# Hand-written order on all engines, V on ScalarE's queue, the late weights behind step 2's V: linear attention and a gated spatial MLP on one core

## The chip, the cores and the metric

The kernel runs on one core of one Trainium2 chip. Times are device microseconds of one execution; the span in a profile is some 1.7 us shorter than the time of the same run. A run over 1.5 per cent above the fastest of its kernel is called slow and left out of ratios. A ratio is the mean time of one kernel's fast runs over that of the other's fast runs of the same rounds, so it is not quite the ratio of the medians quoted beside it.

## The reference, cut to what matters

```python
# attention: q, k, v are (4, 8, 768, 64) float32, lam is one decay per head
intra = (q_b @ k_b.T * Dmask) @ v_b            # inside a block
inter = (q_b * lam_pow) @ kv_state             # from all blocks before
kv_state = lam_block * kv_state + (k_b * rev_pow).T @ v_b
x = out.transpose(0, 2, 1, 3).reshape(4, 768, 512)
# gated MLP with a spatial product over the sequence
h = maximum(x @ w_in, 0)                       # (512, 1024)
u, v = h[..., :512], h[..., 512:]
v_n = (v - mean(v)) / sqrt(var(v) + 1e-6)
v_s = w_spatial @ v_n + b_spatial              # (768, 768) on the sequence
y = (u * v_s) @ w_out                          # (512, 512)
```

Four batches of three steps make twelve steps of 256 tokens. The spatial product of a batch needs all three steps of that batch. That is why the first batch cannot finish before its three steps of K, Q and V (4.7 MB) and the weights (2.95 MB, counted as bf16) have landed.

## The kernel before

Names used in all profile lines (line numbers such as L344 differ from kernel to kernel): `kd`, `qc`, `vc` are the bf16 casts of K (with decay), Q and V. `pt` holds their transposes, evicted as `kT` and `qT`. `pam` is the scores, masked into `a`; `pkv` goes into the state `s` by way of `sd`; `pat` is the attention output, evicted as `xT`. `pv` and `pu` are the two halves of the input projection, evicted as `vh` and `uT`; `st`, `mv`, `rstd`, `vn` are the LayerNorm. `pvs` is the spatial product, gated into `gT`, and `po` the output projection.

All of K, Q and V are issued by SyncE, step by step:

```python
    def load_step(n):
        ...
        for c in range(2):
            nc.sync.dma_start(out=k_in[:, :, c, :], in_=...)
        nc.sync.dma_start(out=q_in..., in_=...)
        for c in range(2):
            nc.sync.dma_start(out=v_in[:, :, c, :], in_=...)
```

Only TensorE and GpSimd are in a written order; a scheduler orders the rest. The weights are issued by GpSimd, all of them ahead of the third step's casts:

```python
    with tc.manual_schedule(engines={PE, mybir.EngineType.Pool}):
        cast_step(0)
        load_win(0, DH)
        cast_step(1)
        nc.gpsimd.dma_start(out=wsp_raw, ...)      # spatial weight
        nc.gpsimd.dma_start(out=bsp_bc, ...)
        nc.gpsimd.dma_start(out=wout_sb, ...)
        trans_step(0); scores_step(0); kv_step(0); trans_step(1)   # (four lines in the source)
        load_step(4)
        fills = {0: 1, 1: 2, 2: 5}
        for n in range(NS):
            if n + 2 < NS:
                cast_step(n + 2)
            ...                                   # loads, scores, output, projections as fills
```

Of the kernel before, what the change touches and what calls it, by code (L numbers as in the profile page):

```python
# [9 lines left out]
FP32 = mybir.dt.float32  # L10
BF16 = mybir.dt.bfloat16
I32 = mybir.dt.int32
AF = mybir.ActivationFunctionType
ALU = mybir.AluOpType
PE = mybir.EngineType.PE
# [3 lines left out]
def kernel(  # L19
# [12 lines left out]
    nc = tc.nc  # L32
    P = 128
    B, H, S, D = q.shape
# [21 lines left out]
    def two_banks(shape, name, dt=FP32):  # L56
        return psum.tile(shape, dt, tag="ps", name=name)


    lam_bc = const.tile([P, H], FP32)  # L60
    nc.scalar.dma_start(out=lam_bc, in_=lam.unsqueeze(0).to_broadcast((P, H)))

    st = {}

    def load_step(n):
        b, r = divmod(n, NR)
        toks = slice(r * T2, (r + 1) * T2)
        q_in = fin.tile([P, H, 2, D], FP32, tag="q_in", name=f"q_in_{n}")
        k_in = fin.tile([P, H, 2, D], FP32, tag="k_in", name=f"k_in_{n}")
        v_in = fin.tile([P, H, 2, D], FP32, tag="v_in", name=f"v_in_{n}")  # L70
        for c in range(2):
            nc.sync.dma_start(out=k_in[:, :, c, :],  # L72
                              in_=k[b, :, toks][:, c * P:(c + 1) * P].rearrange("h p d -> p h d"))
        nc.sync.dma_start(out=q_in.rearrange("p h m d -> p h (m d)"),  # L74
                          in_=q[b, :, toks].rearrange("h (p m) d -> p h (m d)", m=2))
        for c in range(2):
            nc.sync.dma_start(out=v_in[:, :, c, :],  # L77
                              in_=v[b, :, toks][:, c * P:(c + 1) * P].rearrange("h p d -> p h d"))
        st[n] = {"q_in": q_in, "k_in": k_in, "v_in": v_in}

    load_step(0)
    ident = const.tile([P, P], BF16)
    make_identity(nc, ident)

    def iota_f(shape, pattern, base, mult, name):
        ti = const.tile(shape, I32, name=name + "_i")
        nc.gpsimd.iota(ti, pattern=pattern, base=base, channel_multiplier=mult)
        tf = const.tile(shape, FP32, name=name)
        nc.vector.tensor_copy(out=tf, in_=ti)
        return tf  # L90

    krev = iota_f([P, 1], [[0, 1]], P - 1, -1, "krev")

    qpos = iota_f([P, 2, 2, D], [[1, 2], [0, 2], [2, D]], 1, 0, "qpos")

    rel = iota_f([P, 2, D], [[1, 2], [2, D]], 0, -1, "rel")

    win_sb = wpool.tile([P, NCH, DFF], BF16)
    wout_sb = wpool.tile([P, NCH, DM], BF16)
    bsp_bc = wpool.tile([P, S], BF16)  # L100
    wt_sb = wpool.tile([P, NBLK, S], BF16)
    wsp_raw = wpool.tile([P, NBLK, S], BF16)

    def load_win(f0, f1):
        nc.gpsimd.dma_start(out=win_sb[:, :, f0:f1],
                            in_=moe_w_in.rearrange("(g p) f -> p g f", p=P)[:, :, f0:f1])

    load_win(DH, DFF)
    for n in range(1, 4):
        load_step(n)  # L110


    loglam = const.tile([P, H], FP32)
    nc.scalar.activation(out=loglam, in_=lam_bc, func=AF.Ln)
# [3 lines left out]
        nc.vector.tensor_copy(out=logl[rows, :], in_=loglam[rows, hh::2])  # L118
    ldec = const.tile([P, H], FP32)
    nc.scalar.activation(out=ldec, in_=loglam, func=AF.Exp, scale=krev[:, 0:1])  # L120
    lq = const.tile([P, NG, T2], BF16)
    for g in range(NG):
        nc.scalar.activation(out=lq[:, g, :], in_=qpos.rearrange("p m a d -> p (m a d)"),
                             func=AF.Exp, scale=logl[:, g:g + 1])
    l128 = const.tile([P, NG], FP32)
    nc.scalar.activation(out=l128, in_=logl, func=AF.Exp, scale=float(P))
    lm128 = const.tile([P, H], FP32)
    nc.scalar.activation(out=lm128, in_=loglam, func=AF.Exp, scale=-float(P))
    causal = const.tile([P, P], FP32)
    nc.vector.tensor_scalar(out=causal, in0=rel.rearrange("p m d -> p (m d)"), scalar1=0.0,  # L130
                            scalar2=None, op0=ALU.is_ge)
    amask = const.tile([P, 2, 2, 2, P], FP32)
    for h in range(H):
        nc.vector.tensor_scalar(out=amask[:, h // 4, h % 2, (h // 2) % 2, :], in0=causal,
                                scalar1=lm128[:, h:h + 1], scalar2=None, op0=ALU.mult)
    eps_t = const.tile([P, 1], FP32)
    nc.vector.memset(eps_t, 1e-6)
    oo128 = const.tile([P, P], BF16)
    nc.vector.memset(oo128, 1.0 / P)


    xT = {}

    def cast_step(n):
        s = st[n]
        kd = att.tile([P, 2, H, D], BF16, tag="kd", name=f"kd_{n}")
        qc = att.tile([P, 2, H, D], BF16, tag="qc", name=f"qc_{n}")
        vc = att.tile([P, H, 2, D], BF16, tag="vc", name=f"vc_{n}")
        eng = nc.vector if n < NR else nc.gpsimd
        eng.tensor_tensor(out=kd.rearrange("p c h d -> p h c d"), in0=s["k_in"],  # L150
                          in1=ldec.unsqueeze(2).unsqueeze(3).broadcast_to((P, H, 2, D)),
                          op=ALU.mult)
        nc.scalar.activation(out=qc.rearrange("p m h d -> p h m d"), in_=s["q_in"], func=AF.Copy)  # L153
        nc.gpsimd.tensor_copy(out=vc, in_=s["v_in"])  # L154
        s["kd"], s["qc"], s["vc"] = kd, qc, vc

# [112 lines left out]
    def pv(b, r):  # L269
        if r == 0:  # L270
            gmlp_tiles(b)
        x, m = xT[b], gm[b]
        vh, mv, rstd = m["vh"], m["mv"], m["rstd"]
        ps = two_banks([P, 2, DH], f"pv_{b}_{r}")
        for j in range(2):
            for c in range(NCH):
                nc.tensor.matmul(out=ps[:, j], lhsT=x[:, r, c, j * P:(j + 1) * P],  # L277
                                 rhs=win_sb[:, c, DH:DFF], start=(c == 0), stop=(c == NCH - 1))
        pair = slice(2 * r, 2 * r + 2)
        nc.scalar.activation(out=vh[:, pair, :], in_=ps, func=AF.Relu)  # L280
        for t in (2 * r, 2 * r + 1):
            nc.vector.bn_stats(out=m["st6"][:, t, :], in_=vh[:, t, :])  # L282
            nc.vector.bn_aggr(out=mv[:, t, :], in_=m["st6"][:, t, :])
        nc.scalar.activation(out=rstd[:, pair], in_=mv[:, pair, 1], func=AF.Sqrt,
                             bias=eps_t[:, 0:1])
        nc.vector.reciprocal(out=rstd[:, pair], in_=rstd[:, pair])
        for t in (2 * r, 2 * r + 1):
            nc.vector.tensor_scalar(out=m["vn"][:, t, :], in0=vh[:, t, :],  # L288
                                    scalar1=mv[:, t, 0:1], scalar2=rstd[:, t:t + 1],
                                    op0=ALU.subtract, op1=ALU.mult)  # L290
# [45 lines left out]
        nc.scalar.activation(out=wt_sb[:, s:s + 2, :], in_=ps[:, :, 0:S], func=AF.Copy)  # L336


    pend = []

    def fill(n):
        for _ in range(min(n, len(pend))):
            pend.pop(0)()

    def after_out(n):
        b, r = divmod(n, NR)
        pend.append(lambda: pv(b, r))
        if r == 0:
            pend.append(lambda: pu(b, 0))
        if r == NR - 1:  # L350
            pend.append(lambda: pu(b, 1))
            pend.append(lambda: pu(b, 2))
            if b == 0:
                pend.extend([lambda s=s: wt_piece(s) for s in (0, 2, 4)])
            pend.extend([lambda f=f: pvs(b, f) for f in range(NCH)])
            pend.extend([lambda i=i: po(b, i) for i in range(NR)])

    with tc.manual_schedule(engines={PE, mybir.EngineType.Pool}):
        cast_step(0)
        load_win(0, DH)  # L360
        cast_step(1)
        nc.gpsimd.dma_start(out=wsp_raw, in_=moe_w_spatial.rearrange("(a p) s -> p a s", p=P))
        nc.gpsimd.dma_start(out=bsp_bc, in_=moe_b_spatial.unsqueeze(0).to_broadcast((P, S)))
        nc.gpsimd.dma_start(out=wout_sb, in_=moe_w_out.rearrange("(t p) f -> p t f", p=P))
        trans_step(0)
        scores_step(0)
        kv_step(0)
        trans_step(1)
        load_step(4)
        fills = {0: 1, 1: 2, 2: 5}  # L370
        for n in range(NS):
            if n + 2 < NS:
                cast_step(n + 2)
            if n + 5 < NS:
                load_step(n + 5)
            if n + 1 < NS:
                scores_step(n + 1)
            out_step(n)
            after_out(n)
            if n + 1 < NS:  # L380
                kv_step(n + 1)
            f = fills.get(n, 4 + (n % 3 == 0))
            fill(f // 2)
            if n + 2 < NS:
                trans_step(n + 2)
            fill(f - f // 2)
        fill(len(pend))


# [28 lines left out]
```

## Time and profile before

| | kernel before |
|---|---|
| median of the first 4 runs | 185.78 us (185.46 to 186.53) |
| span in the profile | 186.7 us (of a longer run, 188.46 us) |
| V of step 2 cast by GpSimd | 42.0 us, after a wait of 14.4 us |
| first spatial product without a stop (S below) | 66.5 us |
| last matmul ends | 181.5 us |
| work of TensorE per batch at full clock | 33.4 us |

Read it from the middle. From 80 us on TensorE is busy in nearly every slice, so only the opening, up to the first spatial product, has anything large to give. The prediction below shows the lines.

### The profile page before, as it was taken

The numbers are of one execution on the slowest core, as the hardware profiler recorded it, in microseconds if no ns is written. First come the engines' busy times: TensorE is split into PE (matmuls) and PEld (weight loads), VectorE is DVE, ScalarE is ACT, GpSimd is POOL, SyncE is SP. The second block draws the span as 40 slices with busy tenths as digits, with TensorE's granted clock in tenths as the row PEclk, the third lists the DMA queues.
The fourth block names the chain that finished last, engine by engine and source line by source line (L and its number), as shares of the span: only waits on it lengthen the run. The fifth ranks groups of instructions, "written<-read, shape, count | busy, mean of one in ns | idle before, by whom it ended". The sixth has DMA issues, their size and how long they took to land.

```text
span 186.7 us, 3638 instructions
## 1 busy us (share of the span) xinstructions
PE 145.7 (78%) x1540; PEld 96.5 (52%) x1540; DVE 103.4 (55%) x191; ACT 89.1 (48%) x98; POOL 34.8 (19%) x35
## 2 busy tenths in 40 slices
PE   0005677507979779999997999999799999999980
PEld 0005563305649556655776665575676646565430
DVE  1029993705399853542989747169884722564400
ACT  4244324712677942268775613666722157660051
POOL 4004060006245344060606005020000000000000
PEclk9999996975999979999999999999999999999999
DMA  4999969999999999999998900530000027000035
GB/s 98 218 211 252 205 161 184 199 212 232 199 241 248 200 239 238 221 225 222 330 254 195 252 8 0 208 133 4 0 0 4 2 79 262 0 0 4 0 132 205
DMA packets 68337, 28.36 MB, mean 152 GB/s; under 512 B 50528, under 2 KB 65248, under 8 KB 68320
## 3 DMA queue, kind: packets, MB, share of 16 engines
q1 hardware_dynamic: 65664, 25.17, 56.5%
q0 software_dynamic: 2512, 2.95, 9.6%
q8 instruction: 12, 0.20, 0.5%
q14 instruction: 5, 0.04, 0.1%
q10 hardware_dynamic: 144, 0.00, 0.0%
HBM read 24.78 MB, written 6.29 MB: 166 GB/s over the span
## 4 chain that ended last, share of the span: by engine, by line
PE 54%; SPq 13%; DVE 11%; ACT 9%; DMA 9%; issue 2%; POOL 1%; ACTq 0%; POOLq 0%
PE pvs L307 17%; PE po L322 11%; DMA v_in<-in_v_dram 9%; PE pv L277 8%; PE pu L297 7%; SPq L77 6%; SPq L72 5%; PE pt L163 4%; DVE a L192 3%; PE pvs L309 3%; SPq L74 3%; DVE st L282 3%; ACT vh L280 2%; ACT wt_sb L336 2%; DVE vn L288 2%
## 5 line engine op out<-in xcount | busy, mean ns | idle before, releaser
L307 PE MATMUL pvs<-wt_sb,vn 128*128 128x384 bf16 x192 | 37.8, 331 | 2.1 <-ACT wt_sb L336 2.0
L192 DVE TENSOR_TENSOR a<-pam,amask 128x1024 bf16<-128x1024 f32 x24 | 28.5, 1210 | 6.0 <-PE pam L189 6.0
L154 POOL CAST vc<-v_in 128x1024 bf16<-128x1024 f32 x12 | 12.9, 1074 | 84.0 <-DMA v_in<-in_v_dram 42.7
L252 ACT ACTIVATE xT<-pat 128x1024 bf16<-128x1024 f32 x12 | 15.8, 1320 | 23.7 <-PE pat L249 23.6
L307 PEld LDWEIGHTS <-vn 128*128 128x128 bf16 x192 | 18.9, 99 | 14.9 <-issue 2.5
L297 PE MATMUL pu<-xT,win_sb 128*128 128x256 bf16 x192 | 24.4, 285 | 1.9 <-DVE a L192 1.9
L311 DVE TENSOR_TENSOR gT<-pvs,uT 128x768 bf16<-128x768 f32 x16 | 15.3, 958 | 18.2 <-PE pvs L309 18.1
L277 PE MATMUL pv<-win_sb,xT 128*128 128x512 bf16 x96 | 24.2, 400 | 1.2 <-ACT xT L252 1.2
L322 PE MATMUL po<-wout_sb,gT 128*128 128x512 bf16 x96 | 21.9, 379 | 1.5 <-DVE a L192 1.1
L297 PEld LDWEIGHTS <-win_sb 128*128 128x128 bf16 x192 | 19.2, 102 | 5.7 <-issue 1.8
L153 ACT ACTIVATE qc<-q_in 128x1024 bf16<-128x1024 f32 x12 | 12.7, 1055 | 19.0 <-DMA q_in<-in_q_dram 19.0
L325 ACT ACTIVATE o<-po 128x1024 f32<-128x1024 f32 x12 | 12.3, 1025 | 19.0 <-PE po L322 19.0
L282 DVE BATCH_NORM_STATS2 st<-vh 128x6 f32<-128x512 bf16 x24 | 15.6, 682 | 10.4 <-ACT vh L280 10.3
L163 PE MATMUL pt<-ident,kd 128*128 128x128 bf16 x96 | 8.6, 242 | 15.5 <-DVE kd L150 15.5
L170 DVE TENSOR_TENSOR qT<-pt,lq 128x1024 bf16<-128x1024 bf16 x12 | 8.2, 684 | 18.5 <-ACT kT L168 18.5
L150 POOL TENSOR_TENSOR kd<-k_in,ldec 128x1024 bf16<-128x1024 f32 x9 | 17.1, 1897 | 6.1 <-DMA k_in<-in_k_dram 6.1
L168 ACT ACTIVATE kT<-pt 128x1024 bf16<-128x1024 bf16 x12 | 12.2, 1021 | 11.2 <-PE pt L163 11.2
L280 ACT ACTIVATE vh<-pv 128x1024 bf16<-128x1024 f32 x12 | 12.3, 1024 | 8.8 <-PE pv L277 8.8
L163 PEld LDWEIGHTS <-kd 128*128 128x128 bf16 x96 | 7.2, 110 | 17.4 <-DVE kd L150 15.7
L277 PEld LDWEIGHTS <-xT 128*128 128x128 bf16 x96 | 9.5, 102 | 11.7 <-issue 1.7
L322 PEld LDWEIGHTS <-gT 128*128 128x128 bf16 x96 | 9.2, 98 | 11.9 <-issue 1.0
L299 ACT ACTIVATE uT<-pu 128x1024 bf16<-128x1024 f32 x12 | 12.2, 1020 | 5.9 <-PE pu L297 5.8
(52 smaller groups left out, 146.2 us busy)
## 6 DMA issues: line engine op xcount, KB each, us to landing
k_in<-in_k_dram SPq DMA_DIRECT2D x24, 256.0 KB, 5.8
q_in<-in_q_dram SPq DMA_DIRECT2D x12, 512.0 KB, 6.1
v_in<-in_v_dram SPq DMA_DIRECT2D x24, 256.0 KB, 6.0
out_dram<-o SPq DMA_DIRECT2D x12, 512.0 KB, 3.4
wsp_raw<-in_moe_w_spatial_dram POOLq DMA_DIRECT2D x1, 1152.0 KB, 11.3
win_sb<-in_moe_w_in_dram POOLq DMA_DIRECT2D x2, 512.0 KB, 8.4
wout_sb<-in_moe_w_out_dram POOLq DMA_DIRECT2D x1, 512.0 KB, 14.8
bsp_bc<-in_moe_b_spatial_dram POOLq DMA_DIRECT2D x1, 192.0 KB, 11.7
```

Of the source, the lines that this page charges most:

```text
L150: eng.tensor_tensor(out=kd.rearrange("p c h d -> p h c d"), in0=s["k_in"], in1=ldec.unsqueeze(2).unsqueeze(3).broadcast_to((P, H, 2, D)), ...
L154: nc.gpsimd.tensor_copy(out=vc, in_=s["v_in"])
L163: nc.tensor.transpose(out=pt[:, j, g, c * P:(c + 1) * P], in_=src[:, c, 2 * g:2 * g + 2, :].rearrange("p h d -> p (h d)"), identity=ident)
L192: nc.vector.tensor_tensor(out=a_sb[:, i].rearrange("p h g c x -> p (h g) c x"), in0=pam.rearrange("p h g c x -> p (h g) c x"), in1=amask[: ...
L252: nc.scalar.activation(out=xT[b][:, r].rearrange("p g (c d m) -> p (g c) m d", c=2, m=2), in_=po.rearrange("p g c (m d) -> p (g c) m d", m ...
L277: nc.tensor.matmul(out=ps[:, j], lhsT=x[:, r, c, j * P:(j + 1) * P], rhs=win_sb[:, c, DH:DFF], start=(c == 0), stop=(c == NCH - 1))
L280: nc.scalar.activation(out=vh[:, pair, :], in_=ps, func=AF.Relu)
L282: nc.vector.bn_stats(out=m["st6"][:, t, :], in_=vh[:, t, :])
L297: nc.tensor.matmul(out=ps[:, f], lhsT=win_sb[:, c, f * P:(f + 1) * P], rhs=x[:, r, c, :], start=(c == 0), stop=(c == NCH - 1))
L307: nc.tensor.matmul(out=ps[:, i, 0:HW_], lhsT=m["vn"][:, s, f * P:(f + 1) * P], rhs=wt_sb[:, s, cols], start=(s == 0), stop=False)
L311: nc.vector.tensor_tensor(out=m["gT"][:, f, :].rearrange("p (i x) -> p i x", i=2), in0=ps[:, :, 0:HW_], in1=m["uT"][:, f, :].rearrange("p ...
L322: nc.tensor.matmul(out=ps[:, j], lhsT=gT[:, c, t * P:(t + 1) * P], rhs=wout_sb[:, c, :], start=(c == 0), stop=(c == NCH - 1))
```

## The change

The intent is to give every engine a written order. V leaves SyncE's queue for ScalarE's, so that it does not queue behind K and Q. The second half of W_in, the spatial and the output weight go out only after V of step 2 has been cast. TensorE's idle time at the start goes to 48 warm-up matmuls. The Q casts of later steps go to GpSimd, and the LayerNorm is cut in three, so that neighbouring steps can overlap. The core of the diff, cuts marked:

```diff
-        for c in range(2):
-            nc.sync.dma_start(out=v_in[:, :, c, :],
+    def load_v(n):
+        ...
+            nc.scalar.dma_start(out=v_in[:, :, c, :],
...
+    ctx.enter_context(tc.manual_schedule(engines={
+        PE, mybir.EngineType.Pool, mybir.EngineType.Activation, mybir.EngineType.DVE,
+        mybir.EngineType.SP}))
...
+    warm = two_banks([P, 1024], "warm")
+    for i in range(48):
+        nc.tensor.matmul(out=warm[:, 0:P], lhsT=ident, rhs=ident, start=True, stop=True)
...
+        if n < NR:
+            nc.scalar.activation(out=qo, in_=s["q_in"], func=AF.Copy)
+        else:
+            nc.gpsimd.tensor_copy(out=qo, in_=s["q_in"])
...
+    run("""
+        mask c:0 win:1 lk:4 T:0 A:0 lv:2 K:0 O:0 pv:0:0 l0:0:0
+        c:1 lk:5 T:1 l1:0:0 lv:3 A:1 l2:0:0 K:1
+        c:2 win:0 wsp wout lk:6 T:2 O:1 lv:4 A:2 K:2 pv:0:1 l0:0:1
+        pu:0:0 l1:0:1 O:2 pu:0:1 l2:0:1 pv:0:2 pu:0:2 l0:0:2 wt:0 l1:0:2 wt:2 l2:0:2 wt:4
+        c:3 lv:5 c:4 lk:7 pvs:0:0 pvs:0:1 lv:6 T:3 pvs:0:2 A:3 K:3 c:5 pvs:0:3 T:4 po:0:0
+        A:4 O:3 K:4 po:0:1 c:6 po:0:2 lk:8 lv:7 T:5 pv:1:0
+        A:5 O:4 K:5 pu:1:0 c:7 lk:9 lv:8 T:6 l0:1:0 pv:1:1 l1:1:0
+    """)
```

The text is the order of the instructions, each engine taking its own out of it: `lk` loads K and Q, `lv` loads V, `c` casts, `T` transposes, `A` scores, `K` state, `O` output, `l0` to `l2` LayerNorm, `wt` weight transposes, `win`, `wsp` and `wout` the weight loads. In the first row, `lv:2` stands ahead of `O:0` on ScalarE.

## The prediction

> **What bounds the kernel now.** I read the 40 slices first, then the chain of work that ended last, then busy time in stretches that I cut where the character changes, then the timeline of the first 70 us. The slices show two regimes, and the kernel is bound by something else in each:
>
> ```profile
> PE   0005677507979779999997999999799999999980
> PEclk9999996975999979999999999999999999999999
> DMA  4999969999999999999998900530000027000035
> ```
>
> TensorE is half idle in the first third, at 9 in nearly every slice after it, and the DMA row is the reverse. The stretches put numbers on it (columns: width, then busy us and count of PE, PEld, DVE, ACT, POOL, then granted clock, DMA share, GB/s):
>
> ```profile
> 0.00:14.00 14.00, 0.00 (x0) 0.00 (x0) 1.99 (x8) 5.31 (x10) 2.49 (x11) 1.00 0.85 176
> 14.00:26.00 12.00, 8.00 (x116) 7.04 (x118) 11.14 (x21) 3.76 (x6) 3.42 (x4) 1.00 0.97 200
> 26.00:42.00 16.00, 6.68 (x86) 3.63 (x81) 7.49 (x13) 7.26 (x7) 1.57 (x4) 0.83 1.11 204
> 42.00:66.50 24.50, 19.55 (x265) 15.06 (x265) 18.48 (x32) 16.96 (x17) 11.49 (x8) 0.90 1.11 227
> 80.00:114.60 34.60, 33.29 (x377) 22.04 (x376) 23.36 (x44) 20.18 (x23) 8.53 (x7) 1.00 0.81 195
> 114.60:149.20 34.60, 33.30 (x377) 22.23 (x377) 22.44 (x44) 16.66 (x19) 3.55 (x3) 1.00 0.13 47
> 149.20:181.50 32.30, 31.73 (x208) 17.77 (x207) 12.14 (x27) 14.15 (x16) 0.00 (x0) 1.00 0.18 66
> ```
>
> From 80 us to 181.5 TensorE idles 1.3 + 1.3 + 0.6 = 3.2 us in all. There is little to win there. Before 66.5 it is busy 34.2 of 66.5 us, partly at half clock. The timeline names the cause:
>
> ```profile
> 25.44 0.83 POOL L362 DMA_DIRECT2D wsp_raw<-in_moe_w_spatial_dram  x1
> 26.54 10.03 SPq L72 DMA_DIRECT2D k_in<-in_k_dram  x2
> 42.00 1.04 POOL L154 CAST vc<-v_in 128x1024 bf16<-128x1024 f32 x1 [14.43 <-DMA v_in<-in_v_dram]
> 43.09 0.43 PE L207 MATMUL pkv<-vc,kd 128*64 128x64 bf16 x8 [8.07 <-POOL vc L154]
> 66.49 0.48 PE L307 MATMUL pvs<-wt_sb,vn 128*128 128x384 bf16 x2 [1.96 <-ACT wt_sb L336]
> ```
>
> V of step 2 is issued at 24.3, just ahead of the spatial and output weights, and lands at 41.9, with them. VectorE, TensorE and the rest of batch 0 stand still for it; the chain gives it 16 us. The last milestone of the opening is the first spatial matmul, at 66.5, held 2 us by the eviction of the transposed weight. I call its time S.
>
> TensorE's work, from the merged pieces of the chain at full clock: pt 0.89, pam 0.55, pat 1.05 (mean over steps), pkv 0.25, pv 1.73, pu 1.87 and po 1.75 per step, four pvs of 2.27 per batch. One batch: 3 x 8.09 + 9.08 = 33.4, as the 33.3 of the stretches. After S the old kernel owes 109.6 us and takes 115.0 (66.5 to 181.5): 5.4 us go to idle and half clock. The last eviction and store take 5.2 more.
>
> **What the Trainium skill says.** "DMA: Bandwidth & Descriptors", section "Issuing engines are not separate DMA queues": all issuers share the same 16 DMA engines, and spreading saves only issue time. The page's section "Queues, rings and completion order" adds that an engine takes its queue rows in turn, packet by packet. So V on ScalarE's queue brings no bandwidth, but stands in its own row instead of behind K and Q. The trace agrees that rows share: the two W_in halves took 8.1 and 8.7 us each while K, Q and V went on landing. "TensorE: Matmul & The Clock Gate", Part 1: the array runs at half clock until about 3.4 us of activity, and falls back after as long a pause. Here eight transposes take 1.03 us at 14.3 and 0.61 us at 46.8. "ScalarE: Activation LUTs", section "What ACT_TABLE_LOAD costs": about 1283 ns; the trace has 1283 three times, one of them inside the opening (36.4). "GPSIMD Engine Reference", section 1: its SBUF interface is shared with VectorE. The trace fits: a 0.42 us VectorE product (sd) took 2.14 us while GpSimd ran kd.
>
> **The change part by part.**
> (a) V goes to ScalarE's queue and the second W_in half, spatial and output weights are issued only after V of step 2 has landed and been cast. That removes the 16 us wait. But the order has its price: ScalarE is in order, and its V issues carry waits for other loads to land (the order listing resolves them): V1 waits for Q0, V2 for Q1 and K2, V3 for Q3, V4 for K5 and V3.
> (b) 48 warm-up matmuls (about 5 us at half clock, in idle time): at most 1 to 2 us off the first transposes. They are over some 2 us before kd_0, so the array may keep its clock for step 0 only.
> (c) The sqrt table is loaded early: 1.3 us off ScalarE, none of it on the old chain.
> (d) Q casts of steps 3 to 11 move from ScalarE to GpSimd: 9 x 1.06 = 9.5 us off ScalarE, 9 to 13 us onto GpSimd (34.8 busy now), both with room.
> (e) The LayerNorm is cut in three and spread over the order; the last batch's three pu follow its last pv. That covers most idle after 80 us: I take 1 to 2 of the 3.2 us back; the 1.2 us wait for the last gating product at 175.5 stays.
>
> Now S, worked by hand. Bytes counted as they land run at about 0.225 MB/us, 0.46 MB by 4.7 us (first slice). K0 to K2, Q0, Q1, V0, V1 (7 x 0.524) and half of W_in (0.52 as bf16) are 4.19 MB: K2 is in at 4.7 + 3.73/0.225 = 21.3 us. Then ScalarE may issue V2 and only then evicts step 0's attention (xT). From there the written order is serial, since TensorE has pv of step 0 ahead of T1 and VectorE its statistics ahead of kd_1. With the durations of the table: V2 issue 0.7, xT 1.3, pv 3.2 (cold), vh 1.0, statistics 1.7, kd_1 1.2, transposes 1.5, kT 1.0, qT 0.7, scores 0.4, two masks 2.4, vn 1.5, states 1.7, kd_2 1.2, transposes 1.5, kT 1.0, qT 0.7, scores 0.4, masks 2.4, states 0.8 = 26.3, and 1 for twenty hand-overs. Then output 1.1, xT 1.3, pv 1.7, pu 1.9, uT 1.0, three weight evictions of 1.46 and a rstd = 11.7. S = 21.3 + 39 = 60.
>
> Second chain to S: V4's issue stands ahead of vh of step 1 and waits for K5. While W_in's second half lands (29 to 37, measured on the first kernel at 15 to 23.5) the other queues got 0.16 MB/us, while the spatial weight lands about 0.1. Six K and five Q on SyncE's queue are 5.77 MB; by my count K5 is in at 48 to 49. Then 0.8 + vh 1.0 + statistics and rstd 2.1 + xT 1.3 + pv 1.7 + pu 1.9 + uT 1.0 + 4.7 = 14.5: S = 63. If both chains find a warm array and K5 comes at 44, S is 58.
>
> At S the new kernel has done only the first batch's three steps (21.2 us of work: 3 x 2.74 attention, 3 x 3.6 pv and pu, 2.2 weight transposes), where the old one had also started steps 3 and 4 (4.2 us more). It then owes 14.3 + 3 x 33.4 = 114.5. So the span is S + 114.5 + idle 3.5 + tail 5.2 = S + 123.2: 183 for S = 60, 186 for 63, 181 for 58. Against the old: about 4 us earlier S, 4.9 us more work after it, some 2 us less idle.
>
> **Rivals.** First, the removed wait becomes a wait of ScalarE for loads: S at 63 or later and no gain (186). For: the resolved waits, K5 behind 5.8 MB. Against: the order looks tuned to arrivals, and my bandwidth shares are coarse. Second, the weights were the only trouble, the queues keep 0.23 MB/us throughout and the new opening runs at the pace of loads alone: batch 0 needs 4.7 MB and 2.95 MB of weights, at 0.225 landed by 37; with a finishing chain of 15 to 18 us S could be 53 to 55 and the span 177. For: nothing else must be in. Against: steps 3 to 6 share the rings, and the serial chain above takes no notice of bandwidth. Third, TensorE stalls later, by ScalarE's V issues or GpSimd's slower casts: three engine passes of 1.9 + 1.06 + 1.04 = 4.0 us per step against 11.1 of TensorE, so it has slack; 1 to 3 us, up to 189. Fourth, contention for the shared interface makes VectorE late; it is busy 23.4 of 34.6 us, so hidden.
>
> **Range and chances.** My two chains give 183 and 186 of span, 0.6 above the median time. I lean to the lower one, because an order written load by load, with placed waits, was probably fitted to arrivals better than my shares tell, and the second rival can only shorten. I predict 183.0 us, 177 to 188. The 2% line is at 182.4, inside my range: faster 0.45, within 2% 0.47, slower 0.08.
>
> **What would show it.** S itself; GpSimd's cast of V2 before 30 us, without the 14 us wait; a wait of ScalarE or its queue for K2 and K5, of several us, at 15 to 21 and 44 to 49; TensorE idle before T1 and T2; after S, 114 to 119 us to the last matmul; sd no longer next to a GpSimd stall. S below 56 would make me wrong towards fast, and then the serial chain or the waits were shorter than I have them. S above 66, or over 6 us idle after it, would make me wrong towards slow.

## The result, and the profile after

The changed kernel is slower: 203.70 us median of 4 runs (202.43 to 204.76) against 185.78 us. The ratio is 1.0956, with a 95 per cent interval of 1.0866 to 1.1045. The profiled run took 202.43 us, with a span of 200.7.

The slices of the changed kernel, to be laid beside those in the prediction:

```profile
PE   5425060609987799897686689999989999999980
PEclk9955558555999799999999699999999999999996
DMA  3999999999996900059999980068000005200034
```

Two things are new. TensorE has a second weak stretch in slices 18 to 23 (counted from 0, 90 to 120 us), at 6 to 8 where the kernel before stood at 9 all but once. And the DMA engines, which in the kernel before were at 8 or 9 with one break (a 6) from 5 to 107 us, move nothing at 70 to 85 us, with K and Q of four steps still to come.

The stretches of the changed kernel (columns as in the prediction):

```profile
14.00:26.00 12.00, 3.23 (x56) 2.59 (x56) 4.22 (x6) 1.95 (x2) 1.03 (x1) 0.50 1.21 239
26.00:52.00 26.00, 13.51 (x133) 9.06 (x136) 13.45 (x20) 6.48 (x7) 7.61 (x7) 0.60 1.17 223
67.00:84.30 17.30, 16.52 (x178) 10.17 (x179) 9.87 (x13) 3.08 (x4) 7.74 (x6) 0.90 0.19 34
84.30:116.20 31.90, 23.92 (x324) 17.40 (x320) 21.95 (x41) 16.83 (x18) 7.90 (x7) 0.95 1.05 229
116.20:150.80 34.60, 33.11 (x374) 22.16 (x376) 24.14 (x44) 16.58 (x18) 9.21 (x7) 1.00 0.31 80
```

In the opening (14 to 52 us) TensorE does 16.7 us of work in 38, at a granted clock of 0.50 and 0.60. From 84.3 to 116.2 it idles 31.9 - 23.92 = 8.0 us. After that the kernel runs as the one before: 1.5 us idle in 34.6.

The timeline of the changed kernel, lines of ScalarE's queue (ACTq), ScalarE, GpSimd and TensorE:

```profile
16.25 8.37 ACTq L79 DMA_DIRECT2D v_in<-in_v_dram  x2
19.38 1.07 PE L275 MATMUL pat<-a,vc 128*64 128x128 bf16 x16
24.66 1.30 ACT L278 ACTIVATE xT<-pat 128x1024 bf16<-128x1024 f32 x1 [10.02 <-DMA k_in<-in_k_dram]
29.75 1.04 POOL L180 CAST vc<-v_in 128x1024 bf16<-128x1024 f32 x1 [7.67 <-DMA v_in<-in_v_dram]
...
51.75 1.93 ACTq L79 DMA_DIRECT2D v_in<-in_v_dram  x2
53.72 1.02 ACT L306 ACTIVATE vh<-pv 128x1024 bf16<-128x1024 f32 x1 [3.28 <-POOL vc L180]
...
67.02 0.48 PE L344 MATMUL pvs<-wt_sb,vn 128*128 128x384 bf16 x2 [0.85 <-ACT wt_sb L373]
...
109.13 0.29 ACT L317 ACTIVATE rstd<-mv,eps_t 128x2 f32<-128x2 f32 x1 [3.92 <-DVE mv L313]
...
112.11 1.04 PE L215 MATMUL pam<-qT,kT 64*128 64x128 bf16 x16 [3.58 <-DVE qT L196]
```

The 14.4 us wait for V of step 2 is gone: GpSimd casts it at 29.75. In its place ScalarE stands still for 10.02 us ahead of the first `xT`. The attention that `xT` evicts was ready at 20.45, so it is held for the last 4.2 us of these. What ScalarE waits for is K. `xT` needs no K; but the issue of V2 stands ahead of it in ScalarE's stream, and that issue may only go once K2 has landed (24.1 us). The same happens at 51.7, where `vh` of step 1 stands behind V4's issue, and V4's issue behind K5; its matmuls had ended at 52.40, so this hold is 1.3 us. (The line of `vh` names `vc` as what ended the wait; the chain of work goes through K5.) S comes at 67.0, half a microsecond later than before, with 4.9 us less work done by then.

### The profile page after: what moved, and what is told of

It reads as the page before. It is cut to its first block, busy times and chain, and to the rows that moved or that the text cites. A ratio compares the mean times of both kernels' runs of the same rounds, so it can differ in the third digit from the quotient of the medians.

```text
span 200.7 us, 3728 instructions
## 1 busy us (share of the span) xinstructions
PE 152.0 (76%) x1576; PEld 102.0 (51%) x1588; DVE 104.6 (52%) x190; ACT 79.9 (40%) x90; POOL 44.6 (22%) x44
## 4 chain that ended last, share of the span: by engine, by line
PE 44%; DVE 18%; DMA 18%; ACT 8%; SPq 6%; ACTq 2%; issue 2%
DMA k_in<-in_k_dram 18%; PE pvs L344 15%; PE po L359 10%; PE pv L303 8%; DVE a L218 5%; PE pu L334 4%; SPq L68 4%; DVE st L312 4%; PE pvs L346 3%; DVE vn L325 2%; DVE gT L348 2%; ACTq L79 2%; SPq L70 2%; ACT vh L306 2%; PE pt L189 2%
## 5 line engine op out<-in xcount | busy, mean ns | idle before, releaser
L303 PE MATMUL pv<-win_sb,xT 128*128 128x512 bf16 x89 | 23.7, 399 | 7.1 <-ACT xT L278 6.5
L312 DVE BATCH_NORM_STATS2 st<-vh 128x6 f32<-128x512 bf16 x24 | 16.2, 673 | 23.7 <-ACT vh L306 23.7
L348 DVE TENSOR_TENSOR gT<-pvs,uT 128x768 bf16<-128x768 f32 x16 | 15.3, 957 | 18.0 <-PE pvs L346 18.0
L334 PE MATMUL pu<-xT,win_sb 128*128 128x256 bf16 x192 | 22.4, 273 | 0.7 <-DVE a L218 0.7
L334 PEld LDWEIGHTS <-win_sb 128*128 128x128 bf16 x192 | 18.5, 98 | 3.8 <-issue 0.7
L172 POOL TENSOR_TENSOR kd<-k_in,ldec 128x1024 bf16<-128x1024 f32 x9 | 18.2, 2023 | 4.1 <-issue 3.7
L215 PE MATMUL pam<-qT,kT 64*128 64x128 bf16 x192 | 9.1, 246 | 9.8 <-DVE qT L196 9.8
```

What stands on the lines that cost most here:

```text
L172: eng.tensor_tensor(out=kd.rearrange("p c h d -> p h c d"), in0=s["k_in"], in1=ldec.unsqueeze(2).unsqueeze(3).broadcast_to((P, H, 2, D)), ...
L303: nc.tensor.matmul(out=ps[:, j], lhsT=x[:, r, c, j * P:(j + 1) * P], rhs=win_sb[:, c, DH:DFF], start=(c == 0), stop=(c == NCH - 1))
L312: nc.vector.bn_stats(out=m["st6"][:, t, :], in_=vh[:, t, :])
L334: nc.tensor.matmul(out=ps[:, f], lhsT=win_sb[:, c, f * P:(f + 1) * P], rhs=x[:, r, c, :], start=(c == 0), stop=(c == NCH - 1))
L348: nc.vector.tensor_tensor(out=m["gT"][:, f, :].rearrange("p (i x) -> p i x", i=2), in0=ps[:, :, 0:HW_], in1=m["uT"][:, f, :].rearrange("p ...
```

## The experiments

S is the start of the last stop-free run of the first batch's spatial products. "To batch 1" is the time from S to the first spatial product of the second batch; in the changed kernel and all its variants 37.9 us of TensorE's work lie in it. All runs gave correct results.

| kernel | what it is | median us (runs) | ratio to before, 95 per cent | S | to batch 1 |
|---|---|---|---|---|---|
| before | | 185.78 (4) | 1 | 66.5 | 35.6 (less work in it) |
| after | the change | 203.70 (4) | 1.0956 (1.0866 to 1.1045) | 67.0 | 49.1 |
| `b_wlate` | before, weights issued late | 189.80 (4) | 1.0195 (1.0055 to 1.0335) | 67.4 | 33.9 |
| `a_loads` | after, loads ahead of stores | 204.39 (4) | 1.1014 (1.0932 to 1.1096) | 66.5 | 48.1 |
| `a_vsp` | after, V on SyncE | 188.36 (4) | 1.0173 (1.0076 to 1.0270) | 59.0 | 42.2 |
| `a_vsp_order` | V on SyncE, arrivals as in after | 190.15 (4) | 1.0245 (1.0120 to 1.0370) | 58.3 | 45.1 |
| `a_vsp_open` | V0 to V4 on SyncE only | 193.04 (4) | 1.0268 (1.0183 to 1.0353) | 58.3 | 47.9 |
| `a_vsp_early` | `a_vsp`, loads ahead of stores | 188.26 (4) | none | 57.8 | 42.1 |
| `a_qact` | `a_vsp_early`, Q casts on ScalarE | 192.50 (4) | 1.0367 (1.0291 to 1.0443) | 58.6 | 45.4 |
| `a_nowarm` | after, no warm-up | 204.47 (4) | 1.1009 (1.0934 to 1.1083) | 69.0 | 47.2 |
| `a_best` | `a_vsp_early`, reordered | 182.69 (4) | 0.9702 (0.9609 to 0.9794) | 52.8 | 41.7 |
| `a_best2` | reordered further | 174.77 (4) | 0.9305 (0.9233 to 0.9377) | 49.0 | 40.6 |
| `a_fill` | `a_best`, dummy matmuls in waits | 181.25 (4) | none | 48.6 | 42.6 |
| `a_best3` | `a_best2`, dummy matmuls in waits | 179.26 (6) | none | 54.9 | 41.1 |

The last two columns are from the profiled run of each; those of `a_vsp_open` and `a_best3` were slow runs. The median is over all runs, the ratio over fast ones alone: `a_vsp_early` and `a_best` have two of them, `a_fill` and `a_best3` one.

**The theories.** Mine after the first look: ScalarE is an in-order engine, V's issues carry waits for loads to land, and all evictions written behind such an issue wait with it. For the stretch from 84 to 116 us I suspected, besides, that the first three stores stand ahead of K8 on SyncE's queue. The rivals: V now arrives too late because of the order of arrivals; the removed wait would have come back anyway in another load; the warm-up or the slower GpSimd does the harm.

### Is the removed wait worth anything by itself? (`b_wlate`)

```diff
     with tc.manual_schedule(engines={PE, mybir.EngineType.Pool}):
         ...
-        nc.gpsimd.dma_start(out=wsp_raw, ...)
-        nc.gpsimd.dma_start(out=bsp_bc, ...)
-        nc.gpsimd.dma_start(out=wout_sb, ...)
         ...
             if n + 2 < NS:
                 cast_step(n + 2)
+            if n == 0:
+                (the same three)
```

> The first kernel with one part of the change alone: spatial weight, spatial bias and output weight are issued after the cast of V of step 2, not before it. If the 16 us wait for that V was what held the opening, V2 lands by 28 us in place of 41.9, the first spatial matmul comes at 55 to 59 in place of 66.5 and the time falls to 176 to 180. If the rival holds, that the opening runs at the pace of all loads and the weights only change places with K, Q and V, the first spatial matmul stays at 64 or later and the time at 183 to 187.

The chain of work of this run that ended last, in order of time (start, us, what):

```profile
42.54 8.21 DMA q_in<-in_q_dram
...
50.83 1.06 ACT qc L153
...
67.36 0.48 PE pvs L307 x2
```

V2 is cast at 30.47 instead of 42.0, as in the changed kernel, and nothing comes of it: the next loads, V3, K4 and Q4, now share the DMA engines with the weights, and ScalarE, whose order the scheduler made, waits for Q4 with the cast that it had placed ahead of step 2's `xT`. S is 67.4. So the 16 us that the kernel before spent in the wait for V2 were not 16 us to be had. How much of them another order can have, `a_best` and `a_best2` show below.

### The 84 to 116 us stretch: is it the stores? (`a_loads`)

```diff
-        c:3 lv:5 c:4 lk:7 pvs:0:0 pvs:0:1 lv:6 T:3 pvs:0:2 A:3 K:3 c:5 pvs:0:3 T:4 po:0:0
+        c:3 lv:5 c:4 lk:7 lk:8 pvs:0:0 pvs:0:1 lv:6 T:3 pvs:0:2 A:3 K:3 c:5 lk:9 pvs:0:3 T:4 lv:7 po:0:0
```

(and the three words taken out of the two rows below)

> The changed kernel with the K and Q loads of steps 8 and 9 and the V load of step 7 placed ahead of the first output stores. Theory A (the 8 us of idle TensorE between 84 and 116 us come from loads that stand behind the stores in SyncE's queue and are awaited by ScalarE): no load is awaited there any more, that stretch loses 5 to 8 us of idle, time 196 to 199. Theory B (the idle comes from the written order of ScalarE and VectorE at the batch border, whatever the loads do): time 202 to 204, the idle stays at 6 us or more.

The chain of the changed kernel in this stretch had suggested it:

```profile
89.61 7.62 DMA k_in<-in_k_dram
97.25 0.37 ACTq L79
...
97.73 1.03 ACT kT L194
...
104.69 2.80 DVE vn L325 x2
...
109.19 0.37 ACTq L79
...
110.31 1.03 ACT kT L194
```

K8 is issued at 89.61 behind three stores, V8's issue on ScalarE waits for it until 97.25, and step 6's `kT` waits behind V8's issue. With K8 ahead of the stores that piece of the chain is gone. The gain is nothing: 204.39 us. In the timeline of `a_loads` the idle time has only moved on:

```profile
101.54 2.69 DVE L325 TENSOR_SCALAR vn<-vh,mv,rstd 128x512 bf16<-128x512 bf16 x2
...
105.96 0.37 ACTq L79 DMA_DIRECT2D v_in<-in_v_dram  x1
...
114.58 2.08 PE L344 MATMUL pvs<-wt_sb,vn 128*128 128x384 bf16 x6 [3.44 <-DVE a L218]
```

Up to the second batch 1.0 us is won (48.1 against 49.1). It is lost again at once: the spatial products that follow run at half speed here, six in 2.08 and six in 2.12 us, where the changed kernel takes 1.14 for six. That a wait stands on the chain does not say that the time goes with it. This theory fell.

### V back on SyncE's queue (`a_vsp`)

```diff
-            nc.scalar.dma_start(out=v_in[:, :, c, :],
+            nc.sync.dma_start(out=v_in[:, :, c, :],
```

and in the written order each `lv:n` right behind its `lk:n`; ScalarE's stream is otherwise untouched.

> The changed kernel with V back on SyncE's queue, each V after its own K and Q, all else as written. Theory A (ScalarE, in order, waits for loads that its V issues are tied to): its 10 us wait before xT of step 0 and the wait for K5 before vh of step 1 are gone, the first spatial matmuls run without a stop from 60 to 62 in place of 67, time 195 to 199. Theory B (the serial written order binds, the waits lie beside it): first spatial matmuls at 65 or later, time 201 to 205.

The timeline of `a_vsp`:

```profile
18.12 1.30 ACT L277 ACTIVATE xT<-pat 128x1024 bf16<-128x1024 f32 x1 [5.84 <-PE pat L274]
...
59.00 0.48 PE L343 MATMUL pvs<-wt_sb,vn 128*128 128x384 bf16 x2 [0.86 <-ACT wt_sb L372]
```

ScalarE now waits only for TensorE's own result and evicts the first `xT` at 18.12 instead of 24.66. S falls by 8.0 us to 59.0, and the stretch to batch 1 by another 7.0. The time goes from 203.70 to 188.36: this one part of the change makes about 15 of its 18 us of loss, more than I had expected (195 to 199). But two things changed at once, ScalarE's waits and the order in which K, Q and V arrive. Both show in the 6.5 us by which the first `xT` starts earlier: 4.2 are the hold, and the other 2.4 come before it, as Q0 lands earlier with V0 behind it and no longer beside it (its cast starts at 9.09 in place of 11.44).

### Waits or arrivals? (`a_vsp_order`)

V on SyncE's queue, but placed among K and Q in the order in which it had arrived in the changed kernel:

```diff
+    vmid = {1: 1, 2: 2, 5: 4, 6: 5, 7: 6, 8: 7, 9: 8, 10: 9, 11: 10}   # V between K and Q of step n
+    vend = {0: 0, 3: 3, 11: 11}                                        # V behind Q of step n
```

> The changed kernel with V issued by SyncE, but in the order in which V arrived there (V1 between K1 and Q1, V2 between K2 and Q2, V3 after Q3, V4 between K5 and Q5, V5 after K6 and so on), so ScalarE issues no load while the arrivals stay as late. The run with V directly behind its own K and Q had changed both things at once and took S from 67.0 to 59.0 us and the time to 188. Theory A (ScalarE standing still in its V issues, with the evictions behind it, makes the loss): S 58 to 61, no wait of 10 us ahead of step 0's attention output, time 187 to 191. Rival B (the arrival order K, Q ahead of V, a step and more late, makes it): S 64 to 67, GpSimd's cast of V2 near 30 us, time 198 to 204. Mixed: S 61 to 64.

Two lines of its timeline:

```profile
46.43 1.04 POOL L185 CAST vc<-v_in 128x1024 bf16<-128x1024 f32 x1 [5.31 <-DMA v_in<-in_v_dram]
...
58.26 0.48 PE L349 MATMUL pvs<-wt_sb,vn 128*128 128x384 bf16 x2 [0.85 <-ACT wt_sb L378]
```

V3 comes 11 us later than in `a_vsp` (34.99 there), and S does not move: 58.3. So a late V3 is not what costs the opening its 8 us. The run has the order of arrivals and not their times: V1 and V2 are cast at 15.03 and 24.66, in the changed kernel at 21.04 and 29.75. That does not bring the rival back, since the changed kernel first uses these casts at 39.37 and 49.98. But Q0 is early here too (its cast starts at 8.81). So ScalarE's two holds are 4.2 + 1.3 = 5.5 of the 8.0 us by the traces, Q0 is 2.4, and no run has the one without the other. In the next stretch the late arrivals go with 2.9 us (45.1 against 42.2); these are single profiles, and the intervals of the two ratios overlap.

### Does the second loss follow from the first? (`a_vsp_open`)

V of steps 0 to 4 on SyncE, V of steps 5 to 11 left on ScalarE:

```diff
+            eng = nc.sync if n < 5 else nc.scalar
+            eng.dma_start(out=v_in[:, :, c, :],
```

> The changed kernel with V of steps 0 to 4 on SyncE's queue (each behind its own K and Q) and V of steps 5 to 11 left on ScalarE's queue, issued where the changed kernel has them. In the changed kernel S was 67.0 us and from there to the second batch's spatial matmuls 49.2 us; with all V on SyncE 59.0 and 43. If the waits in ScalarE's late V issues (V8's stands behind the first store and K8) make the second loss by themselves: S 59, then 47 to 50, time 193 to 197. If the second loss only follows from the late opening: S 59, then 42 to 44, time 187.5 to 190.

Its S is that of the other two, and the stretch to batch 1 is again near that of the changed kernel, 47.9 us:

```profile
94.86 2.64 DVE L325 TENSOR_SCALAR vn<-vh,mv,rstd 128x512 bf16<-128x512 bf16 x2
...
99.15 0.29 ACT L317 ACTIVATE rstd<-mv,eps_t 128x2 f32<-128x2 f32 x1 [3.75 <-DVE mv L313]
99.21 0.37 ACTq L80 DMA_DIRECT2D v_in<-in_v_dram  x1
...
102.12 1.04 PE L215 MATMUL pam<-qT,kT 64*128 64x128 bf16 x16 [3.42 <-DVE qT L196]
```

The wait of 3.4 to 3.6 us is that of the changed kernel at 112 us and of `a_loads`. The V issue stands there ahead of `vh` and `kT`, but it is not what they wait for: it takes 0.37 and 0.59 us. Ahead of it ScalarE stands still in `rstd`, for statistics that VectorE brings late (3.75 us here, 3.92 and 3.80 in the other two), and VectorE is late because two `vn` take 2.64 us next to GpSimd's `kd` (2.80 and 2.69). In `a_vsp` that `vn` runs clear of `kd` and takes 0.73, `rstd` waits 1.85 and TensorE 1.44 us.

So the 7.0 us between the changed kernel (49.1) and `a_vsp` (42.2) divide like this: TensorE is busy 2.9 us longer, at a lower clock, and idles 4.1 longer. The added idle time stands before the scores of steps 5, 6 and 7, 1.04, 1.47 and 3.58 us against 0.17, 0.18 and 1.44. At the first two, `kT` stands behind the issues of V7 and V8, and `a_loads` shortens them to 0.17 and 0.48; at the third it is VectorE. That the late V puts `vn` and `kd` side by side is not shown.

The profiled run was a slow one. The three fast runs have spans of 189.7 to 192.1 us, a mean of 190.7, against 186.9 for the four of `a_vsp`. That is 3.8 us; by the ratios it is 1.0 per cent, 1.8 us, and their intervals overlap. The two kernels ran on different chips. So V of steps 5 to 11 on ScalarE seems to cost 2 to 4 us by itself, but these runs do not settle it, and they do not part ScalarE's waits from V's later arrival.

### Loads ahead of the stores, once V is on SyncE (`a_vsp_early`)

```diff
-        c:3 c:4 lk:7 lv:7 pvs:0:0 ...
+        c:3 c:4 lk:7 lv:7 lk:8 lv:8 pvs:0:0 ...
-        ... A:3 K:3 c:5 pvs:0:3
+        ... A:3 K:3 c:5 lk:9 lv:9 pvs:0:3
```

> V on SyncE's queue and the loads of steps 8 and 9 ahead of the first stores, both at once. Theory A: the gains add up, time 187 to 192, idle TensorE between the first spatial matmul of batch 0 and that of batch 1 down to 2 us. Theory B: 199 or more.

Its runs fall into two groups, 185.69 and 186.48, 190.03 and 190.59, and the median of 188.26 is that of `a_vsp`. Inconclusive; the profiled run, one of the two fast ones, has a span of 183.9.

### Whose engine should cast Q? (`a_qact`)

```diff
-        if n < NR:
-            nc.scalar.activation(out=qo, in_=s["q_in"], func=AF.Copy)
-        else:
-            nc.gpsimd.tensor_copy(out=qo, in_=s["q_in"])
+        nc.scalar.activation(out=qo, in_=s["q_in"], func=AF.Copy)
```

> The early-load version with V on SyncE (188.3 us median, span 183.9 in its profile), with the Q casts of steps 3 to 11 back on ScalarE as in the kernel before. If GpSimd's extra 1.06 us a step matters (more contention with VectorE[...], later casts of V), the time falls by 1 to 2 us and the statistics products next to a GpSimd cast get shorter. If ScalarE is the engine that sets the pace around 85 to 100 us, as its rstd, kT and xT evictions in the chain suggest, 9.5 us more on it costs 1 to 3 us. I expect the second, 0 to 2 us slower: 188 to 191.

192.50 against 188.26 us: slower by 4 us in the medians, and by 6.4 against the two fast runs of `a_vsp_early` alone, more than expected. Taking the Q casts off GpSimd did not help. It does not test contention as such, since `kd` stays there and two `vn` next to it still take 3.10 us at 102.69. That part of the change is good in this order: 1.06 us more a step on ScalarE is not hidden.

### The warm-up (`a_nowarm`)

```diff
-    warm = two_banks([P, 1024], "warm")
-    for i in range(48):
-        nc.tensor.matmul(out=warm[:, 0:P], lhsT=ident, rhs=ident, start=True, stop=True)
```

> The changed kernel without its 48 warm-up matmuls. They end at 6.8 us and the first transposes start at 9.35 at half speed (1.01 us for eight, as in the kernel before), since the array idles 2.5 us between. So they should do nothing: time within 0.5 us of the changed kernel (203 to 204.5), the first eight transposes 1.0 us as with them. A rival, that they keep the granted clock up for step 0's scores and for the first value projection, would make S 1 us later; a second rival, that early matmuls lower the clock granted at 14 to 52 us (0.50 and 0.60 there, against 0.76 to 1.00 in the kernel before), would raise that clock to 0.8 and make S 3 to 6 us earlier.

The time is the same within the intervals, so the warm-up is no part of the loss, and no gain that these runs can tell. The stretches of this run:

```profile
14.00:26.00 12.00, 5.82 (x62) 3.62 (x64) 4.49 (x6) 1.68 (x2) 1.03 (x1) 1.00 1.26 241
26.00:52.00 26.00, 14.51 (x184) 10.98 (x184) 13.15 (x21) 6.46 (x7) 6.88 (x8) 1.00 1.20 229
```

The granted clock reads 1.00, as the second rival had it. But its eight transposes at 30.77 and at 41.31 us still take 1.03 us each, and S is 2 us later in this run, not 3 to 6 earlier. So the column and the durations contradict each other here, and I go by the durations.

### A version that beats both (`a_best`, `a_best2`)

With V out of ScalarE's way, what orders the opening is VectorE's written order: step 1's K is cast only after the statistics of step 0's projection, which wait for W_in. So I wrote the attention of steps 1 and 2 ahead of them:

```diff
-        mask c:0 win:1 lk:4 lv:4 T:0 A:0 K:0 O:0 pv:0:0 l0:0:0
-        c:1 lk:5 lv:5 T:1 l1:0:0 A:1 l2:0:0 K:1
-        c:2 win:0 wsp wout lk:6 lv:6 T:2 O:1 A:2 K:2 pv:0:1 l0:0:1
+        win:1 mask c:0 lk:4 lv:4 T:0 A:0 K:0 O:0
+        c:1 win:0 lk:5 lv:5 T:1 pv:0:0 A:1 K:1
+        c:2 wsp wout lk:6 lv:6 O:1 T:2 l0:0:0 pv:0:1 A:2 K:2 l1:0:0 l2:0:0
```

and, in the step before the second batch's gating, the transposes of step 7 ahead of the second square root. (The rows after these are adapted.)

> A version meant to beat both: V on SyncE behind its own K and Q with the loads of steps 8 and 9 ahead of the first stores, the first W_in half issued ahead of V0's cast, attention of steps 1 and 2 written ahead of the projections that waited for weights, and in the step before the second batch's gating the last transposes ahead of the second square root. By the serial order S falls from 57.8 to 49 to 53 (VectorE reaches the masks of step 2 at 35 instead of 41.5; the spatial weight lands at about 42), and the two gaps of 1.4 us at 96.7 and 99.8 go. After S the old sum holds, 114.5 of work, some 3 idle and 5.2 of tail: span 172 to 176, time 174 to 178, 5 to 6 per cent under the kernel before. A rival: the loads set S whatever the order, since the spatial weight and K3 land no earlier; then S stays at 56 to 58 and the time at 184 to 187.

182.69 us, 2 per cent under the kernel before in the median and 3.0 by its two fast runs (the other two, at 185, are slow ones), so not yet a clear gain; S is 52.8, right at the edge of what I expected, the time 5 us above it in the median and 2 in its two fast runs. Its trace shows what was left: W_in ahead of V0's cast held Q0 back to 11.5 us, and the fourth spatial product stood behind step 3's scores on VectorE. Both changed, with the spatial weight issued ahead of V2's cast and two more pieces moved:

```diff
-        win:1 mask c:0 ...
+        mask c:0 win:1 ...
-        c:1 win:0 lk:5 ...
+        c:1 win:0 wsp lk:5 ...
-        ... pvs:0:2 A:3 K:3 c:5 lk:9 lv:9 pvs:0:3 T:4 po:0:0
-        A:4 O:3 K:4 po:0:1 ...
+        ... pvs:0:2 pvs:0:3 A:3 K:3 c:5 lk:9 lv:9 T:4 po:0:0
+        po:0:1 A:4 O:3 K:4 ...
-        A:5 O:4 K:5 pu:1:0 c:7 T:6 l0:1:0 ...
+        A:5 O:4 K:5 l0:1:0 pu:1:0 c:7 T:6 ...
```

> The version that beat the kernel before (182.7 us median, span 178.6), with four orders changed: the first W_in half again behind V0's cast (it had delayed Q0 by 3 us), the spatial weight issued ahead of V2's cast, the fourth spatial product ahead of step 3's scores, and the statistics of the second batch's first step ahead of step 6's transposes. By the order S falls from 52.8 to 49 to 51, the 1.22 us gap at 66 and half of the 1.35 us gap at 94.5 go: span 174.5 to 177, time 178 to 181. Rival: the earlier spatial weight pushes V2 and K3 back by as much as it gains, S stays at 52 to 54, time 182 to 184.

174.77 us (173.78 to 175.56), 7.0 per cent under the kernel before and 14 under the changed one, all four runs fast, and better than the 178 to 181 that I expected. TensorE's slices, and one line of its timeline:

```profile
PE   4745694989979989999969999999799999999870
```

```profile
49.00 0.48 PE L343 MATMUL pvs<-wt_sb,vn 128*128 128x384 bf16 x2 [1.32 <-ACT wt_sb L372]
```

By the prediction's own sum: 49.0 + 114.5 + 5.0 idle + 5.2 tail = 173.7, its span, with the idle time as the remainder.

### The half clock in the opening (`a_fill`, `a_best3`)

Dummy matmuls and transposes, whose results are overwritten, in TensorE's waits of steps 0 to 2:

```diff
+    FILL = {0: (24, 40, 24, 24), 1: (6, 10, 0, 28), 2: (24, 0, 0, 8)}
...
+            for _ in range(FILL[n][2] if n in FILL and i == 0 else 0):
+                nc.tensor.matmul(out=pam[:, 0, 0, 0, :], lhsT=ident, rhs=ident, start=True, stop=True)
```

> The version with span 178.6, with dummy matmuls and transposes (180 in all) in TensorE's waits of the opening, so that the array keeps working from 2 to 33 us. If the half clock between 16 and 40 us (0.50 to 0.55) comes from these pauses, the granted clock of that stretch rises to 0.9 and more, eight transposes take 0.61 there instead of 1.03, and S falls by 2 to 4 us: time 179 to 181. If the clock falls for another reason, S and the time stay within 1 us. If the dummies overshoot the waits, S is 1 to 3 us later.

The stretch of `a_best`, and the same of `a_fill`:

```profile
14.00:26.00 12.00, 7.21 (x77) 5.11 (x79) 6.05 (x8) 3.97 (x4) 2.24 (x3) 0.50 1.11 231
```

```profile
14.00:26.00 12.00, 9.90 (x180) 7.78 (x179) 7.93 (x10) 5.32 (x5) 2.19 (x3) 1.00 1.26 243
```

The clock is 1.00 throughout, eight transposes take 0.62 instead of 1.03 us, and S falls by 4.2 us, a little more than expected. The time is not settled: one run of 177.85 us and three between 181.2 and 182.6. On top of `a_best2` the counts were fitted anew (122 dummies):

> The version with 174.8 us median (span 173.7, S 48.5, clock 0.50 to 0.75 from 14 to 40 us), with 122 dummy matmuls and transposes in TensorE's waits of the opening, fitted to the waits of its trace. In the slower version before it such dummies held the granted clock at 1.0 all through and took S from 52.8 to 48.1, but the time by an amount that its runs leave open (one fast run of 177.85 against 179.7 to 185.2). If the half clock costs time on the chain of the opening (a value projection of 3.4 us instead of 1.9, transposes 1.9 instead of 1.05, per step), S falls by 2 to 4 us and the time to 171 to 173.5. If VectorE and the landing loads set the opening, S falls by under 1 us and the time stays at 174 to 175.5.

One run of 170.80 us, the fastest, and five of 178 to 183; the profiled run was one of the slow ones. Neither of the two outcomes that I had written down came. In the profiled run V2 is late again:

```profile
38.66 1.04 POOL L180 CAST vc<-v_in 128x1024 bf16<-128x1024 f32 x1 [14.33 <-DMA v_in<-in_v_dram]
...
39.75 0.43 PE L237 MATMUL pkv<-vc,kd 128*64 128x64 bf16 x8 [8.22 <-POOL vc L180]
```

In `a_best2` V2 was cast at 32.88, with the weights likewise issued ahead. Why it lands later in one run than in another, these runs don't show. Warm matmuls help the opening, but I would not ship this version; `a_best2` is the one that held in all its runs.

## Why the prediction was wrong

I predicted 183.0 us, 177 to 188; it was 203.70. My sum was S + 114.5 + 3.5 + 5.2. What it measured: 67.0 + 114.5 + 13.6 + 5.6 = 200.7, with the 13.6 as the remainder, and the median lies 3.0 above the profiled span. So 7.0 of the error is S, 10.1 the idle time and half clock after S, 0.4 the tail, and the last 3 the step from the span of one run to the median of four. The prediction had this step with the wrong sign: it took the span as 0.6 above the time, by setting the span of a longer run (188.46 us) against the median of others; of one run it is 1.7 below. Both signs that it named for wrong towards slow came, S above 66 and over 6 us idle after it, and it had given "slower" a chance of 0.08.

- **"It then owes 14.3 + 3 x 33.4 = 114.5"** and the tail were right. TensorE's records after S, at full clock, sum to 114.1 us in `a_vsp` and 113.9 in `a_best2`, with a few missing.
- **"That removes the 16 us wait"** was right as an event: V2 was cast at 29.75, before the 30 that I had set as a check. As a gain it was wrong: `b_wlate` removes it and is no faster (2 per cent slower, 0.6 to 3.4).
- **"But the order has its price: ScalarE is in order, and its V issues carry waits for other loads to land"** was the right mechanism, seen before any run. The places were right too, K2 for the first `xT` and K5 for `vh` of step 1. The sizes were short: K2 landed at 24.1 (I had 21.3) and K5 at 51.7 (48 to 49), and from K5 to S it took 15.3 us (14.5). My second chain gave 63 and it was 67.0.
- **"I lean to the lower one, because an order written load by load ... was probably fitted to arrivals"** is where I chose wrongly. I had two chains that both had to end before S, 60 and 63, and S is set by the later one. A belief about who wrote the order is no reason to take the earlier. That one was short too: `vh` of step 1 was held by K5 for only 1.3 us, so without K5 S would have been near 65.7 (an estimate, 67.0 - 1.3), not 60. Of these 5.7 us K2 is 2.8, and 1.1 is a `kd` on VectorE at 32.33 that took 2.29 us next to GpSimd's `kd` (1.22 otherwise); the rest I have not traced.
- **"TensorE stalls later, by ScalarE's V issues or GpSimd's slower casts ... 1 to 3 us, up to 189"** (the third rival) is the step that failed most. Idle and half clock after S came to 13.6 us instead of 3.5. I had set GpSimd's passes, 4.0 us a step, against TensorE's 11.1 and found slack, and had made no such sum for ScalarE, whose V issues I had named. An in-order engine that stands still behind an issue is not even busy, so a sum of busy times would not have shown it. With V on SyncE's queue, 59.0 + 114.5 + 7.6 + 5.2 = 186.3, the span of `a_vsp`: 6.0 us of the 10.1 go with V's queue. The other 4.1 (7.6 - 3.5) stay without it; `a_best2`, with another order, comes to 5.0 in all.
- **"contention for the shared interface makes VectorE late; it is busy 23.4 of 34.6 us, so hidden"** (the fourth rival) was wrong in the 84 to 116 us stretch: two `vn` took 2.80 us at 104.69 next to GpSimd's `kd`, against 0.73 to 0.74 elsewhere, and stood on the chain.
- **The Q casts on GpSimd, "with room"**, were right in direction and too modest: to undo them costs 4 to 6 us in `a_qact`.
- **The warm-up**, "at most 1 to 2 us", fits: no difference in time was found.

What is shown: V on ScalarE's queue makes about 15 of the 18 us (`a_vsp`), and a late V3 is not the cause in the opening (`a_vsp_order`). What is read from the traces, without a run that isolates it: ScalarE's holds as 5.5 of the 8.0 us of the opening and Q0 as 2.4; in the second stretch V issues ahead of `kT`, `vn` next to `kd`, and a lower clock. What is left open: how the second loss divides between ScalarE's waits and V's late arrival.

## What to carry to other kernels

A load issued from an engine that also evicts results is an instruction in that engine's stream: if its issue has to wait, everything written behind it waits too (the first `xT` here, 4.2 us), so put loads that may wait on a queue whose engine has nothing else to do. Before removing the longest wait of a chain, ask which load or engine will be next, and test the removal alone. When an engine waits behind an issue, look one instruction further, at what the engine waited for before it: at 109 us it was VectorE and not the load. Slack of an in-order engine is to be read at the place where its result is needed, not as a share of busy time.

## What the Trainium skill lacked or had wrong

- "DMA: Bandwidth & Descriptors", section "Issuing engines are not separate DMA queues", says that issuing from several engines only saves the sequencer's issue time. It lacks the price: two issues on ScalarE took 8.37 us and held an eviction behind them that had been ready for 4.2 us, and moving V's issues to SyncE took the kernel from 203.70 to 188.36 us.
- "TensorE: Matmul & The Clock Gate", Part 1, gives an idle window of about 3.4 us for the fall to half clock, and I read it as one pause of that length. The page tells of a kernel in which short idle times between groups of matmuls are enough, but gives no length for them. Here, in `a_best2` eight transposes take 0.62 us at 10.00, and 16 scores, after one more wait of 1.84 us, take 1.04 at 12.46, where they take 0.62 when warm. The page also warns that the recorded clock events can be unreliable; `a_nowarm` gives a case, a granted clock of 1.00 over 38 us in which eight transposes took 1.03.
